# Ninth tokens in two half-width chunks, with part of their output stored early: a fused attention and highway kernel on one core

## The chip, the cores and the metric

The kernel runs on one core of one Trainium2 chip. The metric is the device time of one execution in microseconds; where several executions were made it is the median. The profile shows a span (first to last instruction) that is 1.8 to 2.3 us shorter than the device time in the executions here. A ratio between two kernels is the mean of the one's fast executions over the mean of the other's in the same rounds, so it is not quite the ratio of the two medians quoted. Some executions are in a slower state (143 to 146 us here). They are left out of all ratios and no profile is of one; they are counted in the medians, which a single one of them moves by at most 0.1 us, except in e8 (140.44 us with it, 140.11 without).

## The reference

A linear attention is followed by a highway layer. Inputs are float32, the output is 4608 x 512 float32.

```python
# q, k, v: 8 batches, 8 heads, 576 tokens, 64 wide
q_s = softmax(q, over the 64);  k_s = softmax(k, over the 576 tokens)
x = q_s @ (k_s^T @ v)                      # 4608 x 512 after the heads are joined
H = relu(x @ w_h);  T = sigmoid(x @ w_t + b_t)
out = T * H + (1 - T) * x
```

## The kernel before

A batch's 576 tokens are laid out as 64 rows of nine tokens. The first eight tokens of each row make one chunk of 512 columns per batch (chunks 0 to 7). The ninth tokens of all eight batches are gathered in `x9` and make one more chunk, number 8, also 512 columns wide, which is worked on last. For each of four 128-wide output blocks `ob` a chunk goes through a gate, a carry and a blend:

```python
def gate(c, ob):       # 4 matmuls into a PSUM tile, tanh on ScalarE in place
    ps = ps_ht.tile([P, 8, 64], FP32, tag="ht")          # pool of 4 PSUM tiles
    for k_ in range(4): mm(ps, w16["t"][...], xv(k_), ...)
    nc.scalar.activation(ps, ps, AF.Tanh, bias=bt2[...], scale=0.5)

def carry(c, ob):      # 4 matmuls, then dd = max(h, 0) - x on VectorE
    ...
    nc.vector.scalar_tensor_tensor(dd, ps, 0.0, xv(ob), op0=ALU.max, op1=ALU.subtract)

def blend(c, ob):      # g = (tanh + 1) * dd on VectorE, emitted two slots later
    nc.vector.scalar_tensor_tensor(gv(ob), th, 1.0, dd, op0=ALU.add, op1=ALU.mult)
```

TensorE then turns 128x128 blocks of `x + g/2` back to token rows (`out_tile`, 8 matmuls of 128 columns into a PSUM tile), ScalarE or VectorE copies the tile out, and SyncE stores four tiles at a time, 1024 KB. The ninth tokens end the program:

```python
def most9():           # output blocks 0 to 2 of all four batch pairs
    for g in range(4):
        ...            # 6 matmuls of 128 columns
        # g odd: VectorE copies the tile out; g even: ScalarE
    nc.sync.dma_start(rows9[:, :, 0:384], o9[:, :, 0:384])          # 768 KB

def last9():           # block 3 of all four pairs, after the last blend, in one PSUM tile
    ...
    nc.scalar.copy(o9[:, 0:2, 384:512], t[:, 0:2])
    nc.vector.tensor_copy(o9[:, 2:4, 384:512], t[:, 2:4])
    nc.sync.dma_start(rows9[:, :, 384:512], o9[:, :, 384:512])      # 256 KB
```

The order of all engines' work is fixed by hand in slots (`at(p, ...)`); chunk 8 has slots 64 to 71, and the last batch pair's eight output tiles stand two to a slot in slots 65 to 68.

The softmax here doesn't subtract the row's maximum and nothing guards it: scores larger than these inputs give would overflow.

## Time and profile before

| | before |
|---|---|
| device time, median of 3 | 141.24 us (141.20 to 141.51) |
| span of the profiled execution | 139.3 us |
| chunk 8, first matmul | 119.99 us |
| chunk 8, last carry's matmuls begin | 130.05 us |
| last two stores issued (768 KB, 256 KB) | 133.60 and 134.12 us |
| last bytes moved | about 137.7 us |

The table is read from the timeline and from the windows. TensorE's work is one unbroken row until 131.1 us. What follows lasts 8 us, and more than 3 us of it is nothing but output moving to memory.

### The profile page before, as it was taken

Reading aid. Unit: us, or ns where it says so; the run is one execution under the profiler, and the core shown is the slowest. Engines: PE = TensorE matmul, PEld = TensorE weight load, DVE = VectorE, ACT = ScalarE, POOL = GpSimd, SP = SyncE. Lnnn points to the kernel's source line nnn. Section 1 sums busy time; section 2 is a strip of 40 time slices with the busy share of each in tenths; the row PEclk is TensorE's granted clock in tenths of the full one; section 3 lists DMA queues with packets and bytes.
Section 4 is the critical chain, followed back from the end, with each engine's and each line's share of the span. In section 5 each row is a group of like instructions: output and inputs, shape, how many; then the busy total and the mean of one; then the engine's idle time right before and its main releaser. Section 6 shows DMA issues by size and latency. Waiting matters only on the chain.

```text
span 139.3 us, 3531 instructions
## 1 busy us (share of the span) xinstructions
PE 122.2 (88%) x1477; PEld 66.4 (48%) x1477; DVE 106.4 (76%) x200; ACT 88.1 (63%) x126; POOL 44.5 (32%) x37
## 2 busy tenths in 40 slices
PE   4979999967978799969979999999899999999920
PEld 1335344432443355535644754565465455577610
DVE  1395289987998799996996889979977675667840
ACT  3651377719931998639978879769773745565310
POOL 2006003500395429049309701960592000000000
PEclk9999999999999999999999999999999999999997
DMA  4999999999999999935999999950061015077745
GB/s 144 370 388 409 396 387 410 412 412 406 411 412 401 411 410 407 411 132 191 287 412 404 300 328 404 401 224 0 5 261 47 0 75 226 0 285 301 296 159 168
DMA packets 16022, 40.06 MB, mean 288 GB/s; under 512 B 644, under 2 KB 1672, under 8 KB 14984
## 3 DMA queue, kind: packets, MB, share of 16 engines
q1 hardware_dynamic: 16008, 39.85, 74.8%
q8 instruction: 11, 0.18, 0.5%
q14 instruction: 3, 0.02, 0.0%
HBM read 30.41 MB, written 9.44 MB: 286 GB/s over the span
## 4 chain that ended last, share of the span: by engine, by line
PE 50%; DVE 29%; ACT 5%; POOL 5%; DMA 3%; issue 3%; SPq 0%; DVEq 0%; POOLq 0%
PE pt L59 14%; PE ph L59 13%; DVE r L199 12%; PE nat L59 8%; POOL eq L216 5%; PE pq L64 4%; DVE g L305 4%; PE psk L59 3%; DMA q<-in_q_dram 3%; DVE dd L297 3%; PE warm L59 3%; ACT eq L154 2%; DVE eq L212 2%; PE px L59 2%; DVE r L204 2%
## 5 line engine op out<-in xcount | busy, mean ns | idle before, releaser
L288 ACT ACTIVATE pt<-pt,bt 128x512 f32<-128x512 f32 x36 | 23.9, 665 | 29.3 <-PE pt L59 29.3
L216 POOL TENSOR_TENSOR eq<-eq,r 128x1024 f16<-128x1024 f16 (+1 forms) x12 | 25.6, 2153 | 30.2 <-DVE r L204 30.2
L59 PE MATMUL pt<-xT,w16t 128*128 128x512 f16 x128 | 33.3, 380 | 2.1 <-DVE xT L257 1.7
L59 PE MATMUL ph<-xT,w16h 128*128 128x512 f16 x128 | 32.8, 380 | 0.0
L297 DVE SCALAR_TENSOR_TENSOR dd<-ph,xT 128x512 f16<-128x512 f32 x32 | 21.8, 682 | 7.6 <-PE ph L59 7.5
L305 DVE SCALAR_TENSOR_TENSOR g<-pt,dd 128x512 f16<-128x512 f32 x36 | 24.5, 681 | 1.8
L199 DVE TENSOR_REDUCE r<-eq 128x18 f32<-128x1152 f16 x16 | 21.4, 1345 | 4.3 <-ACT eq L154 4.3
L161 POOL CAST v<-v 128x1152 f16<-128x1152 f32 x15 | 16.9, 1147 | 22.7 <-DMA v<-in_v_dram 20.9
L154 ACT ACTIVATE eq<-q 128x1152 f16<-128x1152 f32 x16 | 18.5, 1171 | 2.7 <-DMA q<-in_q_dram 2.7
L154 ACT ACTIVATE ek<-k 128x1152 f16<-128x1152 f32 x16 | 18.4, 1170 | 2.1 <-DMA k<-in_k_dram 2.1
L59 PEld LDWEIGHTS <-w16t 128*128 128x128 f16 x144 | 12.6, 97 | 13.3 <-issue 1.1
L59 PE MATMUL nat<-half_i,g 128*128 128x128 f16 x140 | 18.7, 219 | 0.0
L59 PEld LDWEIGHTS <-w16h 128*128 128x128 f16 x144 | 12.4, 98 | 11.8 <-issue 1.4
L336 ACT COPY o<-nat 128x512 f32<-128x512 f32 x28 | 16.6, 594 | 1.7 <-issue 1.1
L255 ACT CAST xT<-px 128x512 f16<-128x512 f32 x24 | 13.4, 593 | 6.3 <-PE px L59 6.2
L59 PE MATMUL nat<-ident,xT 128*128 128x128 f16 x128 | 17.3, 219 | 0.0
L59 PE MATMUL warm<-wide,ident 128*128 128x512 f16 x52 | 15.3, 444 | 1.9 <-DVE wide L140 1.9
L59 PEld LDWEIGHTS <-g 128*128 128x128 f16 x144 | 14.1, 98 | 3.8 <-DVE g L305 0.4
L233 DVE COPY qsT<-pq 128x1024 f16<-128x1024 f16 (+1 forms) x24 | 12.8, 553 | 3.2 <-PE pq L64 3.0
L59 PEld LDWEIGHTS <-xT 128*128 128x128 f16 x128 | 12.5, 98 | 5.5 <-issue 2.6
L64 PE MATMUL pq<-ident,eq 128*128 128x128 f16 x144 | 11.5, 219 | 2.5 <-POOL eq L216 1.4
L64 PEld LDWEIGHTS <-eq 128*128 128x128 f16 x144 | 8.9, 98 | 6.4 <-POOL eq L216 3.1
(43 smaller groups left out, 84.6 us busy)
## 6 DMA issues: line engine op xcount, KB each, us to landing
out_dram<-o SPq DMA_DIRECT2D x8, 1024.0 KB, 4.8
q<-in_q_dram SPq DMA_DIRECT2D x7, 1152.0 KB, 13.3
k<-in_k_dram SPq DMA_DIRECT2D x7, 1152.0 KB, 14.3
v<-in_v_dram SPq DMA_DIRECT2D x6, 1152.0 KB, 14.7
v<-in_v_dram SPq DMA_DIRECT2D x4, 576.0 KB, 10.7
q<-in_q_dram SPq DMA_DIRECT2D x2, 576.0 KB, 4.1
k<-in_k_dram SPq DMA_DIRECT2D x2, 576.0 KB, 7.1
w32t<-in_moe_w_t_dram SPq DMA_DIRECT2D x1, 1024.0 KB, 13.6
```

Of the source, the lines that this page charges most:

```text
L59: mm = lambda o, l, r, st, sp: nc.tensor.matmul(o, l, r, start=st, stop=sp, skip_group_check=True)
L64: nc.tensor.matmul(o, i, ident, is_transpose=True, start=True, stop=True, skip_group_check=True,)
L154: nc.scalar.activation(dst[b][:, :, 2 * a : 2 * a + 2, :], in32[which][b][:, 2 * a : 2 * a + 2].rearrange("p c n d -> p n c d"), AF.Exp,)
L161: (eng or nc.gpsimd).tensor_copy(v16s[b % 2][:, :, 2 * a : 2 * a + 2, 0:64], in32["v"][b][:, 2 * a : 2 * a + 2].rearrange("p c n d -> p n ...
L199: nc.vector.reduce_sum(qsum[b][:, :, h], eq[b][:, :, h, :], axis=AX.X)
L216: nc.gpsimd.tensor_mul(e, e, r.broadcast_to(list(e.shape)))
L233: nc.vector.tensor_copy(qsT[b][:, :, n0:n1, :], t[:, :, 0:w, :])
L255: nc.scalar.copy(dst, t[c])
L288: nc.scalar.activation(ps, ps, AF.Tanh, bias=bt2[:, ob : ob + 1], scale=0.5)
L297: nc.vector.scalar_tensor_tensor(dd, ps, 0.0, xv(ob), op0=ALU.max, op1=ALU.subtract)
L305: nc.vector.scalar_tensor_tensor(gv(ob), th, 1.0, dd, op0=ALU.add, op1=ALU.mult)
L336: nc.scalar.copy(o, flat(t))
```

## The change

The intent is to have fewer bytes left when the last result is ready. Chunk 8 is cut into chunk 8 (the ninth tokens of batches 0 to 3) and chunk 9 (batches 4 to 7), each 256 columns wide. The first half's output tiles are turned, copied and stored (512 KB) while the second half is worked on. The final stores shrink to 384 KB and 128 KB. To keep TensorE supplied, the last pair's eight output tiles are spread one to a slot.

```diff
-        if c == B:
-            return lambda k_: x9[:, k_], lambda k_: g9[:, k_]
+        if c >= B:
+            h = slice(4 * (c - B), 4 * (c - B) + 4)
+            return lambda k_: x9[:, k_, h], lambda k_: g9[:, k_, h]
 ... gate, carry and dd tiles: 8 -> rows_of(c), which is 4 for the ninth tokens
-    def most9():
 ...
+    def tile9(g, nk):
 ... turn nk blocks of pair g; copy: g even ScalarE, g odd VectorE
+        if g % 2:
+            nc.sync.dma_start(
+                rows9[:, g - 1 : g + 1, 0 : nk * P],
+                o32["9", g // 2][:, 0:2, 0 : nk * P],
+            )
 ... last9: pairs 2 and 3 only; one 128x128 block each for ScalarE and VectorE
-                at(p + 1 + i // 2, E(out_tile, g, i, True))
-    at(8 * B + 8, E(most9), E(last9))
+                at(p + 1 + i, E(out_tile, g, i, True))
+    p = 8 * B + 8
+    at(p + 3, E(tile9, 0, 4))
+    at(p + 4, E(tile9, 1, 4))
+    at(p + 8, E(tile9, 2, 3), E(tile9, 3, 3), E(last9))
```

More of the change, by code (lines that the diff above doesn't have):

```diff
@@ L270, in x_left @@
             nc.vector.tensor_copy(x9v[:, :, c, b, :], t)
+    rows_of = lambda c: 8 if c < B else 4
     def views(c):
-        if c == B:
-            return lambda k_: x9[:, k_], lambda k_: g9[:, k_]
+        if c >= B:
+            h = slice(4 * (c - B), 4 * (c - B) + 4)
+            return lambda k_: x9[:, k_, h], lambda k_: g9[:, k_, h]
         g, b2 = c // 2, c % 2
@@ L284, in gate @@
         xv = views(c)[0]
-        ps = ps_ht.tile([P, 8, 64], FP32, tag="ht", name=f"pt_{c}_{ob}")
+        ps = ps_ht.tile([P, rows_of(c), 64], FP32, tag="ht", name=f"pt_{c}_{ob}")
         for k_ in range(4):
@@ L292, in carry @@
         xv = views(c)[0]
-        ps = ps_ht.tile([P, 8, 64], FP32, tag="ht", name=f"ph_{c}_{ob}")
+        ps = ps_ht.tile([P, rows_of(c), 64], FP32, tag="ht", name=f"ph_{c}_{ob}")
         for k_ in range(4):
             mm(ps, w16["h"][:, k_, ob * P : ob * P + P], xv(k_), k_ == 0, k_ == 3)
-        dd = mo.tile([P, 8, 64], FP16, tag="dd", name=f"dd_{c}_{ob}")
+        dd = mo.tile([P, rows_of(c), 64], FP16, tag="dd", name=f"dd_{c}_{ob}")
         nc.vector.scalar_tensor_tensor(
@@ L345, in blk9 @@
         return t[:, k_, 2 * g : 2 * g + 2].rearrange("p b d -> p (b d)")
-    def most9():
-        o9 = o32["last"] = og.tile([P, 4, 512], FP32, tag="o32", name="o9")
-        for g in range(B // 2):
-            ps, tag = (ps_q, "qx") if g < 3 else (ps_nat, "nat")
-            t = ps.tile([P, 4, P], FP32, tag=tag, name=f"nat9_{g}")
-            for k_ in range(3):
-                turn_block(t, k_, blk9(x9, g, k_), blk9(g9, g, k_))
-            o = o9[:, g, 0:384]
-            if g % 2:
-                nc.vector.tensor_copy(o, flat(t)[:, 0:384])
-            else:
-                nc.scalar.copy(o, flat(t)[:, 0:384])
-        nc.sync.dma_start(rows9[:, :, 0:384], o9[:, :, 0:384])
+    def tile9(g, nk):
+        if g % 2 == 0:
+            o32["9", g // 2] = og.tile([P, 4, 512], FP32, tag="o32", name=f"o9_{g}")
+        t = ps_q.tile([P, 4, P], FP32, tag="qx", name=f"nat9_{g}")
+        for k_ in range(nk):
+            turn_block(t, k_, blk9(x9, g, k_), blk9(g9, g, k_))
+        o = o32["9", g // 2][:, g % 2, 0 : nk * P]
+        if g % 2:
+            nc.vector.tensor_copy(o, flat(t)[:, 0 : nk * P])
+        else:
+            nc.scalar.copy(o, flat(t)[:, 0 : nk * P])
+        if g % 2:
+            nc.sync.dma_start(
+                rows9[:, g - 1 : g + 1, 0 : nk * P],
+                o32["9", g // 2][:, 0:2, 0 : nk * P],
+            )
     def last9():
-        o9 = o32["last"]
+        o9 = o32["9", 1]
         t = ps_ht.tile([P, 4, P], FP32, tag="ht", name="nat9_l")
-        for g in range(B // 2):
-            turn_block(t, g, blk9(x9, g, 3), blk9(g9, g, 3))
-        nc.scalar.copy(o9[:, 0:2, 384:512], t[:, 0:2])
-        nc.vector.tensor_copy(o9[:, 2:4, 384:512], t[:, 2:4])
-        nc.sync.dma_start(rows9[:, :, 384:512], o9[:, :, 384:512])
+        for i in range(2):
+            turn_block(t, i, blk9(x9, i + 2, 3), blk9(g9, i + 2, 3))
+        nc.scalar.copy(o9[:, 0, 384:512], t[:, 0])
+        nc.vector.tensor_copy(o9[:, 1, 384:512], t[:, 1])
+        nc.sync.dma_start(rows9[:, 2:4, 384:512], o9[:, 0:2, 384:512])
     events = {}
@@ L376 @@
     E = lambda f, *a: (lambda: f(*a))
-    for c in range(1, B + 1):
+    for c in range(1, B + 2):
         for ob in range(4):
@@ L382 @@
             at(p + 1, E(carry, c, ob))
-    for c in range(1, B + 1):
+    for c in range(1, B + 2):
         for ob in range(4):
@@ L460 @@
         f()
-    for p in range(8, 8 * (B + 1) + 1):
+    for p in range(8, 8 * (B + 2) + 1):
         for f in events.pop(p, []):
```

## The prediction

> **What bounds the kernel now.** I read the page first (shares of busy time, the 40 slices), then the chain of waits over the last third, then the timeline of the last 20 us, then the stretches (windows) of the last 10 us, then the DMA view.
>
> ```profile
> PE 122.2 (88%) x1477; PEld 66.4 (48%) x1477; DVE 106.4 (76%) x200; ACT 88.1 (63%) x126; POOL 44.5 (32%) x37
> ```
>
> PE is the bound of the body. The diff touches nothing before the last token group's chunk, whose first matmul starts at 119.99 us in the timeline; so only the last 19.3 us can change. The chain of waits says what this stretch is made of:
>
> ```profile
> 120.15 0.86 PE pt L59 x4
> 121.02 0.45 PE nat L59 x8
> ...
> 130.22 0.88 PE ph L59 x4
> 131.09 0.02 issue
> 131.12 0.70 DVE dd L297
> ...
> 131.91 0.70 DVE g L305
> 132.62 0.05 issue
> 132.66 0.58 PE nat_l L59 x7
> 133.24 0.02 issue
> 133.26 0.38 ACT o L366
> 133.64 0.02 issue
> 133.67 0.42 DVE o L367
> ```
>
> Columns are start, length, what. Until 131.09 the chain is PE alone, without a hole: a group of 4 matmuls 512 wide takes 0.865 us, an output tile (8 matmuls 128 wide) 0.445 us. After that comes a serial tail: carry to dd to blend to turning to two copies. Then the timeline shows the two final stores being issued, and the windows show what they do:
>
> ```profile
> 133.60 0.38 SPq L359 DMA_DIRECT2D out_dram<-o  x1
> 133.67 0.42 DVE L367 COPY o<-nat_l 128x256 f32<-128x256 f32 x1
> 134.12 0.41 SPq L368 DMA_DIRECT2D out_dram<-o  x1
> ```
>
> ```profile
> 134.00:134.50 0.50, 0.00 (x0) 0.00 (x0) 0.09 (x1) 0.00 (x0) 0.00 (x0) 1.00 0.00 0
> 134.50:135.00 0.50, 0.00 (x0) 0.00 (x0) 0.00 (x0) 0.00 (x0) 0.00 (x0) 1.00 0.96 350
> ...
> 137.00:137.50 0.50, 0.00 (x0) 0.00 (x0) 0.00 (x0) 0.00 (x0) 0.00 (x0) 0.74 1.05 289
> 137.50:138.00 0.50, 0.00 (x0) 0.00 (x0) 0.00 (x0) 0.00 (x0) 0.00 (x0) 0.50 0.25 70
> ```
>
> The last two columns are the DMA share and GB/s. The queue is empty until 134.5, then full until about 137.65, with every engine idle. That is 768 KB plus 256 KB, 1.05 MB in 3.1 us: 350 GB/s in the 1536-byte rows, 290 in the 512-byte rows. SyncE's wait for the last store runs from 134.6 for 3.34 us to 137.95, 0.3 us after the last byte; from there to the end of the span at 139.3 is 1.35 us of closing work. So the end is set by (a) when the final stores are issued, (b) how many bytes they still carry.
>
> [...] (0.865/4 = 0.216 us at 512, 0.0555 us at 128), so I take 0.109 us at 256, and halving the width costs TensorE nothing that counts. [...] the copies take 0.424 us at 256, 0.550 at 384, 0.692 at 512; the fixed part in the trace is about 0.16 us [...]. [...] VectorE's last copy starts at 133.67, just after ScalarE's of the same tile ended, though PE was done at 133.24 and VectorE's previous copy ended at 133.53. [...] the 768 KB store landed in 3.6 us here [...], the 256 KB store in 4.0 because it queued behind.
>
> **The change, part by part.**
>
> *TensorE.* Removed: 32 matmuls of 512. Added: 64 of 256, so 16 groups of 0.435 = 6.96 us against 8 of 0.865 = 6.92. Turning blocks: 8 output tiles, then 32 blocks of the ninth tokens, in both. No change in the sum. What moves: two complete ninth-token tiles (16 matmuls, 0.89 us) now stand ahead of the last carry, where before all 24 matmuls of the partial tiles stood behind it. The last carry is thus issued completely at 119.99 + 6.96 + (9 + 2) x 0.445 = 131.85; the same sum for before, 119.99 + 6.92 + 9 x 0.445 = 130.92, meets the trace. So +0.93 us to that point.
>
> *VectorE and ScalarE.* Of a halved scalar_tensor_tensor I expect [...] 0.42 us, of a halved tanh 0.665 - 0.22 = 0.44 (the ScalarE copies, 0.594 at 512 and 0.372 at 256, give 0.22). Eight more of each kind-pair: VectorE 16 x 0.42 - 8 x 0.685 = +1.2 us, ScalarE 8 x 0.44 - 4 x 0.665 = +0.9 us. With two half-width groups and two output tiles per 1.76 us of PE, VectorE does two of 0.42 plus one copy of 0.69 = 1.53 us: 87%, still under PE. When I lay the second chunk out, gate 9,2 has to wait for the blend two groups earlier to free its PSUM tile, some 0.05 us; the last carry is then out at about 131.93.
>
> *The serial tail.* Before, carry out (130.91) to end of blend (132.60) took 1.69 us. Now: 0.2 us through PE's pipeline (130.91 to dd's start at 131.12), dd 0.42, with a possible 0.14 behind the previous blend, 0.10 between dependent instructions (131.81 to 131.91), blend 0.42: ends about 133.2. PE's 12 remaining partial-tile matmuls lie beside that. Three turning matmuls after the first, 0.17; pipeline 0.2; ScalarE's 128x128 copy 0.26 (0.372 less 128 elements at 0.87 ns); then, [...] VectorE's 0.29: last store issued at about 134.25. The 384 KB store goes when VectorE has done its 0.55 us copy behind the blend: about 133.70. So the issues are where they were (133.60, 134.12): the later carry eats what the half-width tail saves.
>
> *Stores.* Removed from behind that point: 512 KB. They go at about 131.5 (tile 9,1 out at 130.62, +0.2, copy 0.69), behind the last 1024 KB store, which now issues at about 128.85 instead of 129.28; that one needs 0.7 + 2.5 us to move, the 512 KB another 1.3, so the queue is empty by about 133.8. Then the final burst: 0.9 us from issue to first packet (133.60 to 134.5 before), so from 134.6; 384 KB (0.393 MB) at 350 is 1.12 us, 128 KB at 290 is 0.45; last byte 136.17, landed +0.3 = 136.5, closing 1.35: span 137.8 against 139.3. The sum: -1.57 us of bytes, +0.1 us of issue, -1.5 us. From 141.24 us that is 139.7 us, 1.1% faster.
>
> **The rivals.**
> 1. *A fixed cost takes the place of the bytes.* If a final store took 3.6 us however small it was, 134.25 + 3.6 would end at 137.85, no gain: 141.1 us. Against: the 3.1 us of the final burst are packets in motion, visible in the windows, and only 0.9 + 0.3 around them is not. For: no store under 768 KB is seen alone here. A small share.
> 2. *VectorE becomes the bound.* 87% with dependent steps of 0.10 between them leaves little slack; if PE has to wait for freed PSUM tiles in each group of the second chunk, where no output tiles stand between the last groups (gate and carry together are 0.87 us, dd plus blend 0.94 with gaps), the last carry slips by 0.3 to 0.8 us and the time is 140.0 to 140.5 us. For: VectorE's busy 76% over all, 1.2 us more in this stretch. Against: VectorE had 1.3 us idle before dd and 1.3 before output copies, so the added 1.2 us finds room.
> 3. *The tail is faster than I lay out.* If the last copies do not queue (VectorE's 384-wide copy ahead of the blend's end, say) the issue comes 0.4 us earlier: 139.2 us. More than that would need the whole final burst to vanish, since 2% is 2.8 us and the burst with everything in it is 3.1.
>
> **Range and chances.** Central 139.7. Rivals 2 and 3 give 139.0 to 140.7 as eight in ten. Faster by over 2% needs under 138.4 us: 5%. Slower by over 2% would need a stall of over 4 us from a change of 19 us: 1%. Within 2%: 94%.
>
> **What would show each step.** The changed profile should have 256-wide gate and carry groups of 0.435 us; dd and g of the ninth tokens at 0.42 us and tanh at 0.44; last carry issued near 131.9 instead of 130.9; a 512 KB store issued near 131.5, moved before 133.9; final stores at 133.7 and 134.25; the final burst 1.6 us instead of 3.1. Wrong would be: PE idle above 0.3 us ahead of the second chunk's gates (rival 2), final stores landing 3.5 us or more after issue (rival 1), or final issues before 133.8 (rival 3).

Passages are cut from this text where marked. The forecast's sum came to -1.57 us of bytes and +0.1 us of issue, -1.5 us in all, or 139.7 us. The 0.42 us of a halved VectorE operation: traced figures give the same, 0.685 us less the 0.268 by which the copies at 512 and 256 columns differ (0.692 and 0.424). The 0.109 us of a matmul of 256 columns is an estimate on the line through the traced 0.0555 us at 128 and 0.216 at 512. That VectorE's last copy had to follow ScalarE's was not shown; the trace shows that it did with one tile for both (ScalarE's ended at 133.63, VectorE's began at 133.67), and that of e2, with a tile each, that the two overlapped (ScalarE's from 133.97 to 134.24, VectorE's from 134.08).

## The result, and the profile after

The changed kernel took 140.37 us (140.09 to 140.52, 4 executions) against 141.30 us (141.20 to 141.51, 4 executions): a ratio of 0.993 with a 95% interval of 0.991 to 0.995. That is 0.93 us off the time, within 2%, where 1.5 us had been forecast. The time lies inside the range that was given.

The chain of waits of the changed kernel, its last 8 us (start, length, what):

```profile
130.91 0.69 DVE o L359
131.60 0.34 DVE dd L300
...
132.04 0.42 DVE g L308
132.46 0.34 DVE dd L300
...
132.90 0.44 DVE g L308
...
133.38 0.35 PE nat_l L59 x3
...
133.76 0.27 ACT o L373
...
134.06 0.29 DVE o L374
```

Before, this chain was TensorE until 131.09. Now it is VectorE from 130.91 on: one copy and four half-width operations stand in a row, and the last dd begins 0.36 us after the last carry's matmuls have been issued (they start at 131.58 and take 0.435 us), not 0.2 us. The last blend ends at 133.32, against 132.60 before. SyncE's timeline has the stores:

```profile
131.66 0.38 SPq L363 DMA_DIRECT2D out_dram<-o  x1
...
133.85 0.38 SPq L363 DMA_DIRECT2D out_dram<-o  x1
...
134.37 0.37 SPq L375 DMA_DIRECT2D out_dram<-o  x1
```

The final stores are issued 0.25 us later than before (133.60 and 134.12). So nothing was won by finishing the computing sooner. What was won is in the windows (the last two columns are DMA share and GB/s):

```profile
134.00:134.25 0.25, 0.00 (x0) 0.00 (x0) 0.20 (x1) 0.02 (x1) 0.00 (x0) 1.00 0.06 8
134.50:134.75 0.25, 0.00 (x0) 0.00 (x0) 0.00 (x0) 0.00 (x0) 0.00 (x0) 1.00 0.08 31
134.75:135.00 0.25, 0.00 (x0) 0.00 (x0) 0.00 (x0) 0.00 (x0) 0.00 (x0) 1.00 0.91 332
...
136.00:136.25 0.25, 0.00 (x0) 0.00 (x0) 0.00 (x0) 0.00 (x0) 0.00 (x0) 1.00 1.03 299
136.25:136.50 0.25, 0.00 (x0) 0.00 (x0) 0.00 (x0) 0.00 (x0) 0.00 (x0) 1.00 0.35 97
136.50:136.75 0.25, 0.00 (x0) 0.00 (x0) 0.00 (x0) 0.00 (x0) 0.00 (x0) 1.00 0.06 16
```

The final burst now lasts from 134.75 to about 136.4, some 1.65 us instead of 3.1. Some rows are odd. Before the burst, from 134.0 to 134.7, and after it, from 136.4 to 136.7, the share is 0.06 to 0.08: one DMA engine of the sixteen (one sixteenth is 0.06). The 512 KB store had been issued at 131.66, and one engine was still busy with it when the other fifteen had finished; one engine, presumably the same, also ends the burst last. The store landed 4.1 us after its issue, as slowly as the 1024 KB stores (4.6 in the median). The DMA view of the stretch from 132 to 133 us holds a candidate:

```profile
q8 instruction: 1, 0.02, 5.8%
```

A 16 KB instruction fetch starts there, at 132.75 us, in the packets of the trace, and takes 0.93 us of one DMA engine. The kernel before has no fetch so late: its last is at 122.7 us. The change added 64 instructions to TensorE's stream (from 1477 matmuls and as many weight loads to 1509 of each).

### The profile page after: what moved, and what is told of

It is laid out like the page before. It is cut to its first block, busy times and chain, and to the rows that moved or that the text cites. A ratio compares the mean times of both kernels' runs of the same rounds, so it can differ in the third digit from the quotient of the medians.

```text
span 138.3 us, 3619 instructions
## 1 busy us (share of the span) xinstructions
PE 121.3 (88%) x1509; PEld 69.2 (50%) x1509; DVE 107.2 (77%) x208; ACT 88.8 (64%) x130; POOL 44.6 (32%) x37
## 4 chain that ended last, share of the span: by engine, by line
PE 50%; DVE 30%; ACT 5%; POOL 5%; DMA 3%; issue 3%; SPq 0%; DVEq 0%; POOLq 0%
PE pt L59 14%; PE ph L59 13%; DVE r L199 12%; PE nat L59 9%; POOL eq L216 5%; PE pq L64 4%; DVE g L308 4%; DMA q<-in_q_dram 3%; PE psk L59 3%; DVE dd L300 3%; PE warm L59 3%; ACT eq L154 2%; DVE eq L212 2%; PE px L59 2%; DVE r L204 2%
## 5 line engine op out<-in xcount | busy, mean ns | idle before, releaser
L291 ACT ACTIVATE pt<-pt,bt 128x512 f32<-128x512 f32 (+1 forms) x40 | 24.9, 623 | 27.8 <-PE pt L59 27.7
L308 DVE SCALAR_TENSOR_TENSOR g<-pt,dd 128x512 f16<-128x512 f32 (+1 forms) x40 | 25.2, 630 | 2.4
L59 PEld LDWEIGHTS <-w16t 128*128 128x128 f16 x160 | 14.0, 98 | 12.3 <-issue 1.1
L59 PE MATMUL nat<-half_i,g 128*128 128x128 f16 x142 | 19.8, 219 | 0.1
L154 ACT ACTIVATE ek<-k 128x1152 f16<-128x1152 f32 x16 | 18.4, 1170 | 2.2 <-DMA k<-in_k_dram 2.2
L59 PEld LDWEIGHTS <-w16h 128*128 128x128 f16 x160 | 13.8, 98 | 10.9 <-issue 1.4
L59 PE MATMUL warm<-wide,ident 128*128 128x512 f16 x52 | 14.0, 415 | 1.9 <-DVE wide L140 1.9
```

The costliest lines, as they stand in the source:

```text
L59: mm = lambda o, l, r, st, sp: nc.tensor.matmul(o, l, r, start=st, stop=sp, skip_group_check=True)
L154: nc.scalar.activation(dst[b][:, :, 2 * a : 2 * a + 2, :], in32[which][b][:, 2 * a : 2 * a + 2].rearrange("p c n d -> p n c d"), AF.Exp,)
L291: nc.scalar.activation(ps, ps, AF.Tanh, bias=bt2[:, ob : ob + 1], scale=0.5)
```

## The experiments

Two theories of the gain were set against each other. **Theory:** the end is the start of the final burst plus the bytes still to move. **Rival:** the end is the issue of the last store plus a fixed landing time. A third question came from the result: what does the lagging engine cost, and is the fetch its cause?

The profiled executions differ by up to 1.3 us in when chunk 8 begins, which the change does not touch. So profiles are compared by the stretch from chunk 8's first matmul to the end of the span: 139.3 - 119.99 = 19.3 us before, 138.3 - 120.07 = 18.2 us after. The whole set (the kernel before stands with its values from the rounds of the changed kernel; beside the others its median was 141.32 to 141.43 us):

| run | time, us | ratio to before | chunk start, us | span, us | stretch, us |
|---|---|---|---|---|---|
| before | 141.30 | 1 | 119.99 | 139.3 | 19.3 |
| changed | 140.37 | 0.993 | 120.07 | 138.3 | 18.2 |
| e1_late_store | 141.46 | 1.000 | 120.00 | 139.3 | 19.3 |
| e2_two_banks | 140.37 | 0.994 | 120.40 | 138.8 | 18.4 |
| e3_split_store | 140.23 | 0.992 | 119.88 | 138.2 | 18.3 |
| e4_moved_fetch | 140.46 | 0.992 | 121.13 | 139.1 | 18.0 |
| e5_fetch_late_warm | 140.03 | 0.991 | 119.97 | 137.9 | 17.9 |
| e6_split_banks_fetch | 139.70 | 0.989 | 119.92 | 138.2 | 18.3 |
| e7_before_split | 140.16 | 0.992 | 119.97 | 138.2 | 18.2 |
| e8_bunched_tiles | 140.44 | 0.991 | 120.70 | 138.7 | 18.0 |
| e9_fetch_earlier | 139.61 | 0.987 | 120.03 | 137.6 | 17.6 |
| e10_split_fetch | 139.75 | 0.989 | 120.13 | 137.7 | 17.6 |
| e11_changed_again | 140.27 | 0.992 | 119.94 | 138.2 | 18.3 |
| e12_before_split_again | 140.23 | 0.991 | 119.84 | 138.1 | 18.3 |

All outputs are right. The 95% intervals of the ratios are 0.001 to 0.004 to either side. In the edits below, lines that aren't Python put the code in words.

### e1: all bytes at the end again

```diff
-        if g % 2: store pairs g-1 and g        # 512 KB at 131.7 us, 384 KB at 133.9 us
+        if g == 3: store the 384 KB of pairs 2, 3, then the 512 KB of pairs 0, 1
```

> The changed kernel, with the 512 KB store of the first four batches' ninth tokens issued only behind the 384 KB store; all computing as it was. Theory (the end is the start of the final burst plus the bytes it still carries): the burst is 1.05 MB again and lasts about 2.8 us instead of 1.57; the DMA engine that lagged has nothing to lag behind, which gives back 0.3; so 1.0 to 1.3 us slower than the changed kernel, 141.3 to 141.7 us, no better than before. Rival (the end is the last store's issue plus a fixed landing of 2.7 us): the last issue moves only by one more issue, 0.3 us, so 140.7 us.

The time went back to 141.46 us, level with before (ratio 1.0003). In its windows the queue is empty until 134.5 and works until 137.7, as in the kernel before:

```profile
133.00:134.50 1.50, 0.41 (x5) 0.17 (x3) 1.00 (x3) 0.50 (x2) 0.00 (x0) 1.00 0.00 0
...
137.50:138.00 0.50, 0.00 (x0) 0.00 (x0) 0.00 (x0) 0.00 (x0) 0.00 (x0) 1.00 0.26 72
```

The last store was issued at 134.76 instead of 134.37, 0.39 us later, or 0.46 relative to the chunk's start. The rival therefore allowed about 0.4 us; the stretch grew by 1.1 us. Half-width computing with the bytes left at the end gains nothing: the whole gain of the change is the 512 KB sent early. The rival falls here.

### e2: two PSUM tiles for the last two blocks

```diff
-        t = ps_ht.tile([P, 4, P], FP32, ...)              # one tile for both blocks
+        t = [ps_ht.tile([P, 4, P], FP32, ...) for i in range(2)]
```

> The changed kernel, with the two last 128x128 blocks turned into two PSUM tiles instead of one, so that VectorE's last copy needn't wait for ScalarE's. Expected in the trace: VectorE's last copy starts about 0.25 us earlier and the 128 KB store is issued at about 134.1 instead of 134.37. Theory: that store's packets queue behind the 384 KB ones until about 135.9 anyway, so the time stays at that of the changed kernel within 0.1 us. Rival (the last issue sets the end): 0.27 us faster, 140.1 us.

In the timeline VectorE's copy no longer waits for ScalarE's, but the store behind it does not move (chunk 8 began 0.33 us later here than in the changed kernel):

```profile
134.08 0.29 DVE L374 COPY o<-nat_l 128x128 f32<-128x128 f32 x1
...
134.66 0.41 SPq L375 DMA_DIRECT2D out_dram<-o  x1
```

Relative to the chunk the copy starts 0.31 us earlier (13.68 us after it, against 13.99), and the store is issued at 14.26 against 14.30. SyncE had the 384 KB store to issue first, from 134.18 for 0.38 us. So the wait between the two copies, which the prediction had put into its sum, lay beside SyncE's issue. The expected issue time was missed. As the last issue did not move, this run cannot separate theory and rival. The time was that of the changed kernel, 140.37 us.

### e3: the 384 KB store as two

```diff
-        if g % 2: store pairs g-1, g
+        if g == 1: store pairs 0, 1
+        elif g > 1: store pair g alone          # 192 KB each, the first behind ScalarE's copy
```

> The changed kernel, with the 384 KB store as two of 192 KB, the first issued when ScalarE has copied its tile (about 133.35) rather than when VectorE has copied the second (133.85). Theory: the final burst starts 0.4 to 0.5 us earlier with the same bytes, until the last store's own issue (134.4, first packet 0.9 later, 0.45 of packets) becomes the bound; 0.3 to 0.45 us faster, about 140.0 us. Rival (last issue sets the end): the last issue stays at 134.4 or slips by 0.1, so no gain or 0.1 us slower.

The first 192 KB went at 133.14, which is 13.26 us after the chunk's start, against 13.78 for the 384 KB store. Fifteen engines were done by about 135.7. But the windows go on:

```profile
135.70:135.90 0.20, 0.00 (x0) 0.00 (x0) 0.00 (x0) 0.00 (x0) 0.00 (x0) 1.00 0.08 31
...
136.20:136.40 0.20, 0.00 (x0) 0.00 (x0) 0.00 (x0) 0.00 (x0) 0.00 (x0) 1.00 0.08 23
```

One engine worked on until 136.46. The stretch was 18.3 us, no better than the changed kernel's. The start of the burst had moved as the theory wanted, and the lagging engine had taken the gain. The time was 140.23 us, where 140.0 had been expected. The last issue had not moved either (14.30 us after the chunk's start, as before), so the time alone would fit the rival too; the fifteen engines that were done earlier speak for the theory. It now mattered more what made the sixteenth lag.

### e4: the instruction fetch moved, at the start

```diff
-        E(warm_up, 20),          # 20 matmuls of 512 columns
+        E(warm_narrow, 80),      # 80 matmuls of 128 columns, 120 instructions more
```

> The changed kernel, with the first 20 warm-up matmuls of 512 columns replaced by 80 of 128: the same TensorE time, 120 more TensorE instructions. In the changed kernel a 16 KB instruction fetch falls at 132.8 us, into the moving 512 KB store, and one DMA engine runs on until 136.7 while the rest have ended by 136.4. [...] it moves to about 129 us, when the queue is empty. Theory (that fetch makes one engine lag, and the lag lasts to the end): the trickle of about 20 GB/s after 136.4 goes, landing comes 0.3 us earlier, 140.1 us. Rival (the trickle comes from how the packets of the small stores are dealt out): the trickle stays and the time does not change.

The last fetch fell at 127.65, 6.5 us after the chunk's start instead of 12.7, and not at 129 in an empty queue, as expected, but in a moving 1024 KB store. After the final burst no engine trailed, and SyncE's wait for the last store was 1.9 us instead of 2.2: the 0.3 us that were expected. The time was 140.46 us all the same, and scattered from 139.78 to 141.21. The slowest execution is the profiled one, in which chunk 8 began 1.06 us later than in the changed kernel. The chain of waits shows most of this at about 20 us; this is the changed kernel's row:

```profile
20.30 1.34 DVE w16t L111 x4
```

and this is the same row here:

```profile
20.53 2.17 DVE w16t L111 x4
```

The four casts of the weights took up to 0.84 us each instead of 0.42. Why the casts slowed down was not followed up, and the other three executions have no profile. This run is inconclusive for the time.

### e5: the fetch moved, by later warm-ups

```diff
-        E(warm_up, 6),  ...  E(warm_up, 14),
+        E(warm_narrow, 24),  ...  E(warm_narrow, 56),
```

> The changed kernel, with the warm-up matmuls of two later places (6 and 14 of 512 columns) as 24 and 56 of 128: 120 more TensorE instructions, as in the run before, but the start left alone, where the earlier version lost a microsecond before the chunk began. Theory: the last 16 KB fetch falls 3 to 5 us earlier relative to the ninth-token chunk, the trickle of one DMA engine behind the others goes, last packet to landing as usual: 0.25 to 0.35 us off the stretch from the chunk's first matmul to the end (118.25 us to 138.3 in the changed kernel, seen from its 120.07: 18.23 us, so 17.9). Total 140.1 us if what comes before the chunk stays. Rival (the trickle belongs to the small stores): 18.2 us as before.

(The 118.25 in that text is a slip; the stretch meant is 120.07 to 138.3.) The start was undisturbed, and the last fetch fell at 126.55. The first row is the changed kernel, just after its burst:

```profile
136.45:136.65 0.20, 0.00 (x0) 0.00 (x0) 0.00 (x0) 0.00 (x0) 0.00 (x0) 1.00 0.08 23
```

The second is this run:

```profile
136.45:136.65 0.20, 0.00 (x0) 0.00 (x0) 0.00 (x0) 0.00 (x0) 0.00 (x0) 1.00 0.00 0
```

The trailing engine is gone, the stretch is 17.9 us, and the time 140.03 us (139.92 to 140.11). So an engine that trails at the end of the changed kernel costs 0.3 us, and moving TensorE's instruction stream takes it away. The 0.3 us is read from the profiles (stretches of 18.0 and 17.9 us in e4 and e5, of 18.2 and 18.3 in the changed kernel and e11); in the ratios, 0.991 against 0.992 to 0.993, the intervals overlap.

### e6: split store, two PSUM tiles and moved fetch together

The edits are those of e2, e3 and e5.

> All three together: 384 KB store split in two, last blocks in two PSUM tiles, fetch moved by the later warm-ups. In the run with the split alone 15 engines were done 0.57 us earlier (relative to the chunk's start) while the one that lagged ended where it had, and the time did not move. Theory: with the fetch out of the way the split's gain comes through: the stretch from the chunk's first matmul to the end falls from 18.2 to 17.2 - 17.5 us, 139.3 to 139.6 us in all. Rival (the last store's issue plus 2.7 us sets the end): only what the two PSUM tiles take off the last issue, 0.2 us: 140.1 us.

The median was 139.70 us, 0.1 us above the forecast, but the profiled execution was the slowest of the four (140.18 us), and in it one engine trailed although the fetch had moved to 127.56:

```profile
129.20:129.50 0.30, 0.30 (x7) 0.29 (x6) 0.26 (x1) 0.24 (x1) 0.00 (x0) 1.00 0.06 27
...
135.90:136.20 0.30, 0.00 (x0) 0.00 (x0) 0.00 (x0) 0.00 (x0) 0.00 (x0) 0.50 0.06 19
```

That did not fit "the fetch at 132.75 causes it". The packets of the trace gave a fuller picture. Each of the last stores ends with sixteen packets of 4 bytes in the traces of the two kernels, which I take to be one on each engine. In this execution fifteen engines ended the 1024 KB store that was moving at 127.6 by 128.85, and the sixteenth at 131.36, 2.5 us later. At the end of the next store one was 1.4 us behind, at the very end 0.8. In e5 the numbers were 2.3, 1.2 and nothing. The difference is the pause before the final burst: in e5 and in the changed kernel fifteen engines rest from about 134.0 to 134.7 and the sixteenth makes up all or most of its lag (from 1.2 us to nothing in e5, from 1.3 to 0.3 in the changed kernel); the split store fills that pause.

That a fetch makes an engine lag can be checked on two earlier stores of 1024 KB in all fourteen traces, as moving TensorE's stream also moved the earlier fetches. Of the store that ends at about 117 to 118 us, the last engine is 1.7 to 2.1 us behind in the four runs with a fetch in it (e4, e5, e6, e10) and at most 0.04 in the other ten. Of the next one, which ends at 125 to 126 us, it is at most 0.03 us behind in these four, 0.8 to 2.0 in the nine runs with a fetch in it, and 0.4 in e9, whose fetch begins just as the others end. In e1 the last fetch fell in the pause before the final burst, at 132.62, and no engine trailed that burst.

### e7: the kernel before, with smaller stores alone

```diff
-            if g % 2: VectorE copies, else ScalarE
+            if g > 1: VectorE copies, else ScalarE
+            if g % 2: store pairs g-1, g            # two of 384 KB
-        nc.sync.dma_start(rows9[:, :, 0:384], o9[:, :, 0:384])   # 768 KB
```

> The kernel before (full-width chunk), with smaller final stores alone: ScalarE copies the partial tiles of the first two pairs and VectorE those of the last two, and the 768 KB store becomes two of 384 KB, the first issued as soon as ScalarE is done, at about 132.65 instead of 133.60. Theory (the end is the start of the final burst plus its bytes): the burst of 1.05 MB starts at about 133.5 instead of 134.5, so 0.9 to 1.0 us faster than before, 140.3 to 140.4 us: as much as the whole change brings, without halving anything. Rival (the gain of the change needs the bytes sent early by halving the chunk; last issue sets the end): the last issue stays at 134.1 to 134.2, no gain, 141.3 us.

This is the kernel before, at full width. SyncE's timeline has the first and the last of its three final stores:

```profile
132.36 0.38 SPq L360 DMA_DIRECT2D out_dram<-o  x1
134.10 0.37 SPq L371 DMA_DIRECT2D out_dram<-o  x1
```

and its windows show the burst from about 133.25 to 136.5:

```profile
133.20:133.40 0.20, 0.01 (x1) 0.00 (x0) 0.20 (x1) 0.16 (x1) 0.00 (x0) 1.00 0.63 230
...
136.40:136.60 0.20, 0.00 (x0) 0.00 (x0) 0.00 (x0) 0.00 (x0) 0.00 (x0) 0.50 0.57 156
```

The burst carries the same 1.05 MB as before; it starts 1.25 us earlier and ends 1.1 us earlier. The last store was issued at 134.10, as before (134.12), so the rival allowed nothing. The time was 140.16 us (ratio 0.992). One edit in the copies and one in the stores brings what the whole change brings.

### e8: output tiles two to a slot

```diff
-                at(p + 1 + i, E(out_tile, g, i, True))
+                at(p + 1 + i // 2, E(out_tile, g, i, True))
```

> The changed kernel, with the last batch pair's eight output tiles placed two to a slot, as in the kernel before, instead of one to a slot: the half-width groups after the fourth slot then have no output tiles between them. Theory (half-width groups alone are bound by the turnround of their PSUM tiles: dd 0.42, blend 0.42 and 0.3 of waits between a carry and the gate two groups on, 1.2 us, against 0.87 of TensorE): about 0.3 us of TensorE idle in each of some five groups, the last carry 1.0 to 1.6 us later, 141.4 to 142.0 us. Rival (VectorE had the room, the placing does not matter): within 0.2 us of the changed kernel.

The theory of this run was wrong. The last carry began 132.27 - 120.70 = 11.57 us after the chunk's start, against 131.58 - 120.07 = 11.51 in the changed kernel, and the fast executions took 140.07 to 140.77 us (140.11 in the median). Two rows of the timeline, of TensorE and of VectorE, where no output tiles stand between the groups:

```profile
128.26 0.60 PE L59 MATMUL pt<-x,w16t 128*128 128x256 f16 x4
...
128.28 0.42 DVE L308 SCALAR_TENSOR_TENSOR g<-pt,dd 128x256 f16<-128x256 f32 x1
```

The first row is the gate of chunk 9, block 0, the second the blend of chunk 8, block 2, two blocks before it. If there were only the four PSUM tiles that I had counted, the gate would have had to wait until that blend ended at 128.70. It did not: four tiles' room seems to hold more than four half-width tiles, though this was not looked into further. In the chain of waits the gates and carries follow each other at 0.44 us with a single hole of 0.05. VectorE keeps up, with a dd and a blend every 0.86 us (dd at 127.76, 128.62, 129.48 and 130.34). Placing the output tiles one to a slot was not needed for the gain. The last fetch fell late here too, at 132.34, as the 512 KB store was issued; one engine ended that store 0.8 us behind but had caught up by the end. So the lag of a late fetch need not reach the end.

### e9 and e10: the last fetch at two places

e9 is e6 with all 32 later warm-up matmuls made narrow (192 more instructions instead of 120); e10 is e6 unaltered, in the same rounds.

> Split 384 KB store and two PSUM tiles as before, with all 32 later warm-up matmuls as 128 narrow ones: 192 TensorE instructions more than the changed kernel instead of 120. In the last such run the moved fetch fell at 127.6 us, in a 1 MB store; one DMA engine finished that store 2.5 us after the others and was still 0.8 us behind at the end, because the split store leaves no pause in which it could catch up. Theory (each fetch sets one engine back by 1.5 to 2.5 us, pauses in the stores make it good): the last fetch moves to about 124 to 125 us, the engine has caught up by the 512 KB store, all 16 engines end together at about 135.7; span about 137.3 us for a chunk that starts at 120.0, 139.3 us in all. Rival (the split store itself is dealt unevenly, whatever the fetch does): one engine again ends 0.8 us after the others, 139.7 us or more.

> The kernel of the earlier run (split store, two PSUM tiles, 120 more TensorE instructions) again on this chip beside the last one, so that the two differ only in where the last instruction fetch falls. Theory: one engine 0.8 us behind at the end again, and about 0.5 to 0.8 us slower than its neighbour. Rival: the same time and the same lag in both.

In e9 the fetch fell at 125.6. One engine ended the store behind it 1.0 us after the others and the next within 0.1 us, and at the end all sixteen were done by 135.8:

```profile
135.90:136.20 0.30, 0.00 (x0) 0.00 (x0) 0.00 (x0) 0.00 (x0) 0.00 (x0) 0.83 0.00 0
```

The stretch is 17.6 us and the time 139.61 us (fast executions 139.35 to 139.66). That is 0.987 of the kernel before, with an interval of 0.985 to 0.989: the fastest version tried, though not clear of e10. The 512 KB store landed 2.8 us after its issue here (4.1 in the changed kernel). The last store was issued 14.18 us after the chunk's start, only 0.12 us earlier than in the changed kernel, while the stretch is 0.7 us shorter, which again speaks against the rival of the last issue. For e10 I expected an engine 0.8 us behind and a loss of 0.5 to 0.8 us, and both were missed. The fetch was again at 127.9, one engine was again behind, by 1.7 us after that store and 0.6 after the next, but it had caught up by the end. The time was 139.75 us, with overlapping intervals. So how far a fetch sets an engine back differs from execution to execution of one kernel (2.5 us in e6, 1.7 here); to judge by the times (139.49 to 139.94 us in eight of the nine executions of e6 and e10, 140.18 in the other), in most executions the pauses of the split version suffice.

### e11 and e12: the change and e7 side by side

> The changed kernel unaltered, beside the next one, to compare the two on one chip in the same rounds. Both theories: 140.2 to 140.5 us.

> The kernel before with the split 768 KB store alone, again, beside the changed kernel. Theory (two equal gains by two ways: bytes sent early, or the same bytes started earlier): 140.1 to 140.3 us, level with the changed kernel or 0.1 to 0.3 us better, because it has no late instruction fetch and no engine left behind. Rival (the earlier comparison, made on another call, flattered it): more than 0.3 us slower than the changed kernel.

In the same rounds the changed kernel took 140.27 us (ratio 0.9917) and e7 140.23 us (0.9914). They are level. In the profile of the changed kernel one engine trails the burst by 0.3 us again; in that of e7 none does.

## Why the prediction was right or wrong

**The bound.** Right. The gain is the final burst. e1 put 512 KB back into it and lost all of the gain; e7 left the bytes and started them earlier and gained the same.

**TensorE.** Right, but for one detail: the 0.05 us wait of gate 9,2 for a PSUM tile is not in the trace (e8 suggests why: more than four half-width tiles found room). The half-width groups took 0.44 us, and the last carry's matmuls were all issued at 131.58 + 0.435 = 132.02, which is 131.94 when the 0.08 us later start of the chunk is taken off; 131.93 was forecast with that wait, 131.85 without it.

**VectorE and ScalarE.** The sizes were right: 0.41 to 0.42 us for dd and blend, 0.45 for tanh. VectorE's row of operations at the end (copy, dd, blend, dd, blend) put the last dd 0.36 us behind the last carry, as the "possible 0.14" had allowed, and the last blend ended at 133.32 against "about 133.2".

**The serial tail.** The issue times were 0.15 and 0.12 us later than forecast (133.85 and 134.37 against 133.70 and 134.25), of which 0.08 is the chunk's start. One reason in it was wrong: VectorE's wait for ScalarE in the shared PSUM tile (0.27 us in the changed kernel) was counted as part of the path to the last issue. e2 took it away and the issue moved by 0.04 us, because SyncE was still issuing the store ahead of it. The terms of this sum also give 134.1 and not 134.25; the gaps between the instructions, 0.13 us in the profile before, are not named in it.

**Stores.** The mechanism was right and one term of the sum was mis-sized. What failed is "last byte 136.17, landed +0.3 = 136.5". Fifteen engines ended at about 136.4: of this 0.15 us is the later issue (with the chunk's 0.08), and the burst took 1.65 us where 1.57 had been forecast. The sixteenth ended at 136.7. The DMA view gives the last store 2.7 us from issue to landing, so it landed at 137.1, 0.4 us after the last packet. The same step failed a little earlier: "the queue is empty by about 133.8" became 134.1 for fifteen engines, and the one behind them was at work on the 512 KB until after 135. e5 measured what that engine costs: 0.3 us. Of the half microsecond between the forecast span (137.8) and the measured one (138.3), the chunk's start is 0.08, the later issue and the longer burst about 0.15, and the engine 0.3.

Some slips in the prediction change little. SyncE's wait for the last store was put at 134.6 to 137.95; that is the first start of several instructions on one line, and the long wait ended at 138.1 (issue at 134.12, landing 4.0 us later). So landing takes 0.4 us after the last packet, not 0.3, and the closing work 1.2, not 1.35; in the sum the two nearly cancel. "-1.57 us of bytes" is the burst that stays; 3.1 - 1.57 = 1.53 us go. In rival 3, 139.7 less 0.4 is 139.3. The sign for it, "final issues before 133.8", contradicts the forecast of 133.70 for the 384 KB store and can be meant for the last store only.

**The rivals.** A fixed cost in place of the bytes: refuted by the landings, 2.9 and 2.7 us after issue where 3.5 or more would have been its sign, and by e1 and e7. VectorE as the bound: it did become the last part of the chain, but it moved the last carry by nothing that the profile of the change shows, and by at most 0.06 us in e8. A faster tail: not in the change; a split store and an undisturbed DMA queue bring it (e9, 1.8 us under the kernel before in the medians).

**Left open.** The trace does not number the DMA engines, so that the fetch and the lag sit on the same engine is inferred: a share of 0.06 is one engine, and a lag arises in the stores with a fetch in them and, apart from what is carried over, not in the others. It is also open why a fetch of 0.9 to 1.9 us (0.93 in the changed kernel, 1.9 in e5) leaves an engine 0.8 to 2.5 us behind, and why the weights' casts slowed down in e4.

## What to carry to other kernels

When a kernel ends in a burst of stores, count the bytes in the burst and look when its first store is issued: here the end moved with these two (512 KB more cost 1.1 us in e1, a start 1.25 us earlier gained 1.1 in e7) and not with the last store's issue. Before restructuring the computing to send bytes early, see whether part of the finished output is merely waiting for a slower copy behind one large store; here a changed share of the copies and a split store gave as much as halving the chunk (140.23 and 140.27 us in the same rounds). And when a DMA share of one sixteenth trails before or after a burst (0.06 to 0.08 here, a cost of 0.3 us), look for an instruction fetch in the stores ahead of it.
